# A linear-attention block with a gated MLP on one core: the rest of q formed beside k, the reciprocal denominator spread by DMA, the gate's tiles on 128 rows around the folds, and the last tile in column parts

## The chip, the cores and the metric

The kernel runs on one core of one Trainium2 chip. The time is the device time of that core in microseconds (us), as a median of several runs. The "span" that the profile gives is the profiled part of one run, and it is 1.7 to 2.2 us shorter than that run's time. A run of one kernel that is over 1.5% above the fastest of that kernel counts as slow and is left out of comparisons.

Names of engines in the profile: PE is the matrix engine, PEld its weight loads, DVE the vector engine, ACT the scalar engine, POOL the third elementwise engine, SP the engine whose queue issues most DMAs (SPq is that queue). SBUF is the memory that the kernel's tiles lie in, up to 128 partitions each, PSUM the banks that its matmuls write.

## The reference, cut to what matters

```
B, S, D, F, H = 1, 2048, 448, 1792, 16        # head size Dh = 28, bf16

xn = layernorm(x)

# A: linear attention
q, k, v = heads(xn @ wqkv)
phi     = lambda t: where(t > 0, t + 1, exp(t)) + 1e-6
kv      = einsum("bhsd,bhse->bhde", phi(k), v)
z       = einsum("bhsd->bhd", phi(k))
num     = einsum("bhqd,bhde->bhqe", phi(q), kv)
den     = einsum("bhqd,bhd->bhq", phi(q), z) + 1e-6
s       = (num / den) @ wo

# B: the gate
g   = silu(relu(xn @ w1 + b1) ** 2 @ w2 + b2)

out = x + s * g
```

`den` has one number per token and head. It divides the 28 features of that head, so 1/den has to be spread from 16 heads to 448 features before it can multiply phi(q).

## The kernel before

The program lists its operations in the order in which PE is to run them, and a small scheduler places those of the other engines. D = 448 is 3 x 128 + 64 rows, so a product over D takes seven steps of 64 rows. The kernel runs two products at once, one on the upper and one on the lower 64 rows (in the trace, at L852, the second of two such matmuls starts 0.003 us after the first, and 28 of them, 448 columns each, take 2.65 us). A `phase` is such a pair of products; `K4` and `K3` are the four and three steps of a half:

```
half = (slice(0, 64), slice(64, 128), slice(0, 128))
K4, K3 = (3, 0, 1, 2), (0, 1, 2)
...
def kk(si):                       # k of one tile of 128 tokens: 448 columns
    ...
        return e.matmul(
            ps(b)[:, 0:D], xT[half[h], c, si * P : (si + 1) * P], w_qkv[half[h], c, D : 2 * D], start=start,
            stop=stop,
        )
...
def q_rest(pair):                 # q's features 384..447, two groups of 512 tokens, a product of its own
    ...
        for i in (0, 1):
            g = 2 * pair + i
            last = e.matmul(
                ps(b)[half[i], 0:512], w_qkv[half[h], c, 384:448], xT[half[h], c, g * 512 : (g + 1) * 512],
                start=start, stop=stop,
            )
```

`den()` leaves the denominators of four groups of 512 tokens in a PSUM bank, group g at partitions 32g to 32g+15, one head per partition. ACT makes 1/den of it (`rden`, a log and an exponential). Then PE spreads it: `spread` multiplies `rden` with a matrix of zeros and ones, and DVE multiplies phi(q) with the result.

```
def spread(*what):
    ...
        for h, (g, r) in enumerate(what):
            w = ehd[half[h], g % 2, r * P : (r + 1) * P] if r < 3 else ehr[half[h], :, :]
            last = e.matmul(ps(bufs[h])[:, 0:512], w, rden[half[h], :], start=True, stop=True)
    ...
    add("pe", f, ["rden", "ehd", "ehr"], bufs, 0.22)
    for (g, r), b in zip(what, bufs):
        ...
        add("dve", lambda e, _, sl=sl, b=b: e.tensor_tensor(out=sl, in0=sl, in1=ps(b)[:, 0:512], op=ALU.mult), ...)
```

`fold_wv` and `fold_wo` fold the state kv with the weights, so that s becomes one product of phi(q)/den with `msb`: `ss` (called an S phase here). `gg` is the gate's second product, over F = 14 x 128 rows (called g). The order on PE, cut:

```
r0, r1 = q_rest(0), q_rest(1)
phase((r0, K4), (r1, K4))
phase((r1, K3), (r0, K3))
token_sum(0); z_heads(); token_sum(1); den(); token_sum(2); token_sum(3); fold_wv()
...
phase((h8, K4), (h11, K4))
spread(*todo.pop(0))
phase((h9, K4), (h12, K4))
...
phase((ga, A), (gb, A))
spread(*todo.pop(0))
phase((ga, B), (gb, B))
...
ss_columns(15, 0)
ss_columns(15, 1)
```

## Time and profile before

| What | Value |
|---|---|
| time, median of the first 3 runs | 147.88 us (147.73 to 148.08) |
| span of the profiled run | 146.1 us |
| PE busy | 141.3 us, 97% |
| PE waits in the whole run | 1.3 us, one, at the start |
| first hidden-layer matmul to last matmul | 9.65 to 142.5 us, without a gap |

The page of the kernel before: busy time by engine, the rows of PE and of its granted clock in 40 slices of the span (9 is 90% or more), and the chain of waits by engine.

```profile
PE 141.3 (97%) x1330; PEld 69.2 (47%) x1330; DVE 97.2 (67%) x224; ACT 79.8 (55%) x154; POOL 21.2 (14%) x39
...
PE   6999999999999999999999999999999999999990
...
PEclk9999999999999999999999999999999999999999
...
PE 93%; DVE 3%; DMA 2%; issue 0%; DVEq 0%
```

The waits of PE in the kernel before (engine and line, what it waited for; total us, times, longest):

```profile
PE pb L966 <- DVE junk L341: 1.3, 1, 1.3
```

Read together, these say that the matrix engine bounds the kernel. The chain that ended last is PE work for 93% of the span, PE has one short wait, and its clock is on record as full (1.00) from 5.6 to 145.5 us, past its last matmul, which ends at 142.8. By this profile, shortening DVE or ACT would gain nothing; taking matmuls away would.

The groups of instructions by form in the kernel before (line, engine, operation, shapes, count; busy us and mean ns of one; idle time before them):

```profile
L601 PE MATMUL pb<-w_qkv,xT 64*128 64x448 bf16 x100 | 14.6, 349 | 0.0
...
L839 DVE TENSOR_TENSOR pqT<-pqT,pb 128x512 bf16<-128x512 bf16 x12 | 7.7, 684 | 3.1 <-PE pb L830 3.1
...
L830 PE MATMUL pb<-rden,ehd 64*128 64x512 bf16 x12 | 2.3, 376 | 0.0
...
L638 PE MATMUL pb<-xT,w_qkv 64*64 64x512 bf16 x28 | 1.9, 383 | 0.1
```

L601 is k, L638 the separate product of q's rest, L830 the spreading of 1/den, and L839 the DVE product that uses it. The mean of one matmul (349 ns) is not its cost on PE, because matmuls overlap. From start to start in the trace, a 448-column matmul takes 0.189 us, one of 512 columns 0.216, and a change of tile shape to or from one with 64 or 32 rows or columns adds about 0.094 (a 448-column matmul before such a change takes 0.283).

The chain of waits of the kernel before, between 66 and 83 us (start, us, what):

```profile
66.06 1.02 PE pb L638 x16
...
67.12 0.84 PE pb L638 x12
67.97 3.13 PE pb L683 x16
...
78.55 1.63 PE pb L689 x16
...
82.20 0.22 PE pb L830 x2
```

The rest of q costs 1.02 + 0.84 us of the chain, and each pair of spreading matmuls 0.22.

### The profile page before, as it was taken

The numbers are of one execution on the slowest core, as the hardware profiler recorded it, in microseconds if no ns is written. First come the engines' busy times: TensorE is split into PE (matmuls) and PEld (weight loads), VectorE is DVE, ScalarE is ACT, GpSimd is POOL, SyncE is SP. The second block draws the span as 40 slices with busy tenths as digits, with TensorE's granted clock in tenths as the row PEclk, the third lists the DMA queues.
The fourth block names the chain that finished last, engine by engine and source line by source line (L and its number), as shares of the span: only waits on it lengthen the run. The fifth ranks groups of instructions, "written<-read, shape, count | busy, mean of one in ns | idle before, by whom it ended". The sixth has DMA issues, their size and how long they took to land.

```text
span 146.1 us, 3240 instructions
## 1 busy us (share of the span) xinstructions
PE 141.3 (97%) x1330; PEld 69.2 (47%) x1330; DVE 97.2 (67%) x224; ACT 79.8 (55%) x154; POOL 21.2 (14%) x39
## 2 busy tenths in 40 slices
PE   6999999999999999999999999999999999999990
PEld 2344446644444446443545535545555555555440
DVE  0979688888978995999995594973052341604583
ACT  3557799889887888889797191613030220301310
POOL 6000000000000000008900000000050505144140
PEclk9999999999999999999999999999999999999999
DMA  4997649995301100000000000000001011020122
GB/s 124 307 332 215 161 88 350 307 204 112 72 4 36 36 4 0 0 0 4 0 0 0 4 0 0 7 0 0 0 17 51 31 36 63 0 65 2 63 94 94
DMA packets 15513, 10.54 MB, mean 72 GB/s; under 512 B 7244, under 2 KB 15116, under 8 KB 15500
## 3 DMA queue, kind: packets, MB, share of 16 engines
q1 hardware_dynamic: 15040, 9.89, 26.5%
q10 hardware_dynamic: 460, 0.46, 0.9%
q8 instruction: 10, 0.16, 0.5%
q14 instruction: 3, 0.02, 0.1%
HBM read 6.94 MB, written 1.84 MB: 60 GB/s over the span
## 4 chain that ended last, share of the span: by engine, by line
PE 93%; DVE 3%; DMA 2%; issue 0%; DVEq 0%
PE pb L651 29%; PE pb L852 29%; PE pb L601 7%; PE pb L912 7%; PE pb L683 6%; PE pb L623 6%; DMA x_tok<-in_A_x_dram 2%; PE pb L638 1%; DVE st L447 1%; PE pb L689 1%; PE pb L830 1%; PE pb L775 1%; PE pb L741 1%; PE pb L803 1%; PE pb L930 1%; PE pb L490 1%
## 5 line engine op out<-in xcount | busy, mean ns | idle before, releaser
L651 PE MATMUL pb<-xT,w 64*128 64x512 bf16 x392 | 51.6, 376 | 0.1
L852 PE MATMUL pb<-w,r 64*128 64x448 bf16 x448 | 48.2, 349 | 0.0
L660 ACT ACTIVATE r<-pb,b1f 128x512 bf16<-128x512 f32 x56 | 35.0, 689 | 9.0 <-PE pb L651 8.9
L852 PEld LDWEIGHTS pb<-w,r 64*128 64x128 bf16 x448 | 22.8, 94 | 21.0 <-PE pb L852 0.6
L651 PEld LDWEIGHTS pb<-xT,w 64*128 64x128 bf16 x392 | 21.7, 94 | 21.7 <-ACT r L660 0.7
L870 ACT ACTIVATE gbuf<-gbuf 128x448 bf16<-128x448 bf16 x15 | 8.3, 577 | 35.7 <-DVE gbuf L860 35.7
L860 DVE TENSOR_TENSOR gbuf<-pb,b2b 128x448 bf16<-128x448 f32 x15 | 8.7, 621 | 25.4 <-PE pb L852 25.4
L899 POOL TENSOR_TENSOR obuf<-obuf,x_tok 128x448 bf16<-128x448 bf16 x12 | 12.1, 1029 | 57.4 <-DVE obuf L889 57.4
L601 PE MATMUL pb<-w_qkv,xT 64*128 64x448 bf16 (+1 forms) x106 | 16.0, 350 | 0.0
L623 PE MATMUL pb<-xT,w_qkv 64*128 64x512 bf16 x84 | 15.6, 376 | 0.0
L668 DVE TENSOR_TENSOR r<-r 128x512 bf16<-128x512 bf16 x37 | 13.7, 443 | 0.0
L912 PE MATMUL pb<-msb,pqT 64*128 64x448 bf16 x90 | 13.6, 349 | 0.0
L669 ACT ACTIVATE r<-r 128x512 bf16<-128x512 bf16 x19 | 11.3, 633 | 0.0
L447 DVE BATCH_NORM_STATS2 st<-x_tok 128x6 f32<-128x448 bf16 x16 | 9.4, 611 | 2.5 <-DMA x_tok<-in_A_x_dram 2.5
L889 DVE TENSOR_TENSOR obuf<-pb,gbuf 128x448 bf16<-128x448 f32 (+1 forms) x17 | 9.6, 593 | 2.2 <-PE pb L852 1.7
L579 ACT ACTIVATE pk<-pb 128x448 bf16<-128x448 f32 x16 | 8.1, 540 | 3.6 <-PE pb L601 2.9
L591 DVE SCALAR_TENSOR_TENSOR pk<-pb,pk 128x448 bf16<-128x448 f32 x16 | 9.8, 622 | 0.4
L378 POOL MEMSET ehd<- 128x896 bf16 x1 | 0.8, 844 | 62.9 <-DVE zb L613 62.9
L839 DVE TENSOR_TENSOR pqT<-pqT,pb 128x512 bf16<-128x512 bf16 x12 | 7.7, 684 | 3.1 <-PE pb L830 3.1
L683 PE MATMUL pb<-pk,xn 128*128 128x448 bf16 x48 | 9.6, 353 | 0.0
L601 PEld LDWEIGHTS pb<-w_qkv,xT 64*128 64x128 bf16 (+1 forms) x106 | 6.8, 94 | 5.1 <-DVE xT L500 0.4
L623 PEld LDWEIGHTS pb<-xT,w_qkv 64*128 64x128 bf16 x84 | 6.3, 94 | 4.3
(90 smaller groups left out, 117.5 us busy)
## 6 DMA issues: line engine op xcount, KB each, us to landing
out_dram<-obuf SPq DMA_DIRECT2D x15, 112.0 KB, 1.7
w<-in_B_w_dram SPq DMA_DIRECT2D x1, 1568.0 KB, 9.5
x_tok<-in_A_x_dram SPq DMA_DIRECT2D x3, 448.0 KB, 4.4
w_qkv<-in_A_wqkv_dram SPq DMA_DIRECT2D x3, 336.0 KB, 4.8
w<-in_B_w_dram SPq DMA_DIRECT2D x2, 384.0 KB, 4.6
w<-in_B_w_dram SPq DMA_DIRECT2D x1, 576.0 KB, 5.7
w_o<-in_A_wo_dram SPq DMA_DIRECT2D x1, 392.0 KB, 10.8
w_qkv<-in_A_wqkv_dram SPq DMA_DIRECT2D x6, 56.0 KB, 4.3
```

The costliest lines, as they stand in the source:

```text
L447: "dve", lambda e, _: e.bn_stats(st6[:, si, :], x_tok[:, si, :]), [("x", si)], [("st", si)], 0.553
L591: lambda e, _: e.scalar_tensor_tensor(out=slot, in0=ps(buf)[0:rows, 0:n], scalar=1.0 + 1e-6, in1=slot, op0=ALU.add, op1=ALU.max),
L601: return e.matmul(ps(b)[:, 0:D], xT[half[h], c, si * P : (si + 1) * P], w_qkv[half[h], c, D : 2 * D], start=start, stop=stop,)
L623: return e.matmul(ps(b)[:, 0:512], w_qkv[half[h], c, m * P : (m + 1) * P], xT[half[h], c, g * 512 : (g + 1) * 512], start=start, stop=stop,)
L651: return e.matmul(ps(b)[:, 0:512], w_1[half[h], c, fi * P : (fi + 1) * P], xT[half[h], c, g * 512 : (g + 1) * 512], start=start, stop=stop,)
L660: lambda e, _: e.activation(out=slot, in_=ps(b)[:, 0:512], func=AF.Relu, bias=b1f[:, fi : fi + 1]),
L668: return e.tensor_tensor(out=slot, in0=slot, in1=slot, op=ALU.mult)
L669: return e.activation(out=slot, in_=slot, func=AF.Square)
L683: last = e.matmul(ps(b)[:, 0:D], xn[:, si, c * P : (c + 1) * P], pk[:, si, :], start=(si == 0), stop=(si == NT - 1),)
L852: return e.matmul(ps(b)[:, 0:D], r2[half[h], fi, si * P : (si + 1) * P], w_2[half[h], fi, :], start=start, stop=stop)
L899: eng, lambda e, _: e.tensor_tensor(out=ob, in0=ob, in1=x_tok[:, si, :], op=ALU.add),
L912: return e.matmul(ps(b)[:, 0:D], q, msb[half[h], k, :], start=start, stop=stop)
```

## The change

The intent is to take work off PE. There are four parts.

1. **q rest beside k.** The k product of a token tile gets 64 more columns, q's features 384 to 447. They come out with tokens on partitions, so a DMA transposes them, two tiles at a time. The separate q-rest product goes.
2. **1/den spread by DMA.** Four DMAs write `rden` to DRAM. Each reads 16 partitions (the 16 heads of a group) and repeats each row 28 times. Six DMAs read the result back as 128 partitions of features. The spreading matmuls go.
3. **g on 128 rows around the folds.** Where the neighbours are products on 128 rows, the gate's tiles 0 to 3, 14 and 15 also run on 128 rows, which avoids changes of tile shape at 0.094 us each.
4. **The last tile in column parts**, 256 and 192 columns, to shorten the end.

The diff, cut to its core:

```
 def kk(si):
-    ps(b)[:, 0:D], xT[half[h], c, si * P : (si + 1) * P], w_qkv[half[h], c, D : 2 * D], start=start,
-    stop=stop,
+    ps(b)[:, 0:512], xT[half[h], c, si * P : (si + 1) * P], w_qkv[half[h], c, 384 : 2 * D],
+    start=start, stop=stop,
...
+def rest_transpose(pair):
+    add("sp", lambda e, _: e.dma_start_transpose(out=pqR[:, pair * P : (pair + 1) * P], in_=qk[:, pair, 0:P]), ...)
...
-def q_rest(pair):
...
-def spread(*what):
...
+def scale_q():
+    for g in range(NG):
+        rows = rden[32 * g : 32 * g + NH, :]                                     # 16 partitions
+        rows = bass.AP(tensor=rows.tensor, offset=rows.offset, ap=[rows.ap[0], [0, DH], rows.ap[1]])   # each row 28 times
+        dma("sp", spread[:, g * 512 : (g + 1) * 512].rearrange("(h j) t -> h j t", h=NH), rows, [("spread", g)], D * 1024, ["rden"])
+    for g in range(NG):
+        dma("sp", rb[:, :, g * 512 : (g + 1) * 512], spread[0:384, g * 512 : (g + 1) * 512]..., [("rb", g)], 384 * 1024, [("spread", g)])
+        if g:
+            continue
+        for i in (0, 1):
+            dma("sp", rbR[half[i], :]..., by_parity(spread[384:448, :], i), [("rbr", i)], 64 * 2048, [("spread", k) for k in range(NG)])
+    for g in range(NG):
+        ...   # DVE: pqT *= rb (3 x 512 columns at once), pqR *= rbR
...
-r0, r1 = q_rest(0), q_rest(1)
-phase((r0, K4), (r1, K4))
-phase((r1, K3), (r0, K3))
+full(gg(0))
+full(gg(1))
+z_heads(); token_sum(0); den(); open_gates(); scale_q()
+token_sum(3); token_sum(1); token_sum(2)
+full(gg(2))
+fold_wv()
+full(gg(3))
...
+for i, *pairs in ((4, 0), (6, 2), (8, 4, 6), (10, 8), (12, 10, 12)):
+    ga, gb = gg(i), gg(i + 1)
+    ...
+    phase((ga, C), (gb, C))
+    phase((x, K4), (y, K4))       # the first S phase
...
+full(gg(15, ca))
+full(ss(15, ca, eng="dve", end=False), KS, ["msz"])
+full(gg(15, cb, True), range(NF + 1))
+full(ss(15, cb, eng="dve", end=False), KS, ["msz"])
```

The two small reads of `spread[384:448]` need all four writes, because they take the last 64 features of every token group. Every S phase needs the scaled rest of q, so every S phase needs the last of the four writes.

## The prediction

> What bounds the kernel. TensorE. The table of busy time has PE at 141.3 of 146.1 us (97%), the chain of waits is 93% PE, and PE's waits add up to 1.3 us, all at the start. From the first hidden-layer matmul (9.65 us) to the last matmul (142.5 us) PE never stops, at full granted clock. So only removed PE work, a shorter tail or a new PE stall can move the time; DVE (67%) and ACT (55%) have room.
>
> PE work, from start-to-start times in the timeline: a 448-column matmul 0.189 us, 512 columns 0.216, 224 columns 0.096, 112 columns 0.052, alike on 128 rows and on a pair of 64-row halves; a change of tile shape adds 0.094. [...]
>
> Removed: the separate q-rest product, 1.9 us (blocks of 1.02 and 0.84); seven pairs of broadcast matmuls, 7 x 0.216 = 1.5; about 0.2 of the z product; ten of sixteen shape switches, 0.9 (partly in the items above); small waits around the folds and the last tiles, 0.3 to 0.4. Added: k tiles of 512 instead of 448 columns, 56 slots x 0.027 = 1.5, 0.17 of it in the head; two half slots for tiles 14 and 15 on zero-padded weights, 0.2. These spacings applied to every matmul of both programs give -2.7 us after the head; with head and waits, PE ends 2.6 to 3.0 us earlier. The tail (142.6 to 146.1) shrinks 0.1 to 0.2. Net about -3.1 us: 144.8 if nothing stalls.
>
> Not on the path: q scaling on DVE (14 x 0.684 us become four 3x512 products of about 0.9); longer k evictions; removed POOL constants.
>
> What may stall. 1/den now goes through DRAM and back: four writes of 448 rows of 1 KB, each read from 16 partitions, then four reads of 384 KB and two small ones that need all the writes. 1/den is there near 83 us, and the first S phase should start near 99.3. At 46 ns per 1 KB packet and engine (the trace's own reads) everything lands by 96, some 2 us to spare. [...] I hold the stall a little less likely than not.
>
> Prediction: 145.2 us, range 144.2 to 152.0; faster by over 2% 0.36, within 2% 0.37, slower by over 2% 0.27. The no-stall case lies on the 2% line.
>
> What would show each step: PE matmuls 1330 to 1215; q-rest and broadcast groups gone; no PE idle before the first S matmul (right), or a wait there on DVE's scaled q, itself on the DMA into rb (wrong); [...] DVE's min-add on k still near 270 ns; tail near 3.3 us.
>
> Wrong if: the DRAM round trip is late; DVE or ACT fall behind in the k phases so that PE waits for PSUM banks; the DMA transposes of q rest delay the next xT.

The sum without a stall came to 144.8 us. The case with a stall came to 151 to 153 us; all its terms were worked out from a transfer rate that no DMA of the trace of before showed. The stated 145.2 us lies between the two cases, near the first.

## The result, and the profile after

| | before | after |
|---|---|---|
| time, median | 147.98 us (147.73 to 148.15, 4 runs) | 155.84 us (154.85 to 157.19, 4 runs, the 157.19 slow) |
| ratio of fast runs | | 1.051 (95%: 1.048 to 1.055), slower |
| span of the profiled run | 146.1 us | 153.1 us |
| mean granted clock of PE | 0.998, full until 145.5 us | 0.965 |

Ratios in this document are the mean time of one kernel's fast runs over the mean of the other's fast runs of the same rounds, to within 0.0002, so they are not quite the ratio of the medians beside them. The outputs of every experiment were correct.

The page of the changed kernel, the same parts as before, with its line of DMA issues for the new writes at the end (KB each, median us from issue to landing):

```profile
PE 140.3 (92%) x1215; PEld 67.6 (44%) x1215; DVE 91.2 (60%) x218; ACT 78.9 (52%) x151; POOL 23.5 (15%) x37
...
PE   6999999999999999999999999900899999999992
...
PEclk9999999999999999999999999975589999999999
...
PE 80%; DMA 12%; SPq 4%; DVE 1%; ACT 1%; issue 0%; DVEq 0%
...
spread<-rden SPq DMA_DIRECT2D x4, 448.0 KB, 13.1
```

The matmuls went down from 1330 to 1215 as planned. But the row of PE now has two slices of nothing, the row of the clock reads 7, 5, 5, 8 from the first of these slices on, and the chain of waits holds 12% DMA and 4% of the issuing queue, where it had 2% and none.

The waits in the changed kernel, of DVE and of PE:

```profile
DVE pqT L850 <- DMA xT<-spread: 12.6, 2, 11.2
...
PE pb L955 <- DVE pqR L856: 8.4, 1, 8.4
...
PE pb L994 <- DVE junk L345: 1.3, 1, 1.3
```

Apart from the 1.3 us at the start, PE waits once, for 8.44 us, at the first S phase (L955), for DVE's scaled rest of q (`pqR`). DVE itself had waited for the DMA that reads `spread` back (into the space of `xT`). So the engine named in PE's wait is not the cause; the DMA behind it is. DVE's queue adds to it: its scaling of the first group waited 11.2 us for a read that landed at 104.83, and the copies of the folded weights, which the S phase needs too, stood behind it and ended at 107.41.

The chain of waits of the changed kernel across that stall (start, us, what):

```profile
82.19 0.64 ACT rden L819
...
84.30 3.89 SPq L393
...
88.23 15.52 DMA spread<-rden
...
103.76 0.57 SPq L393
...
104.37 3.10 DMA xT<-spread
...
107.50 0.30 DVE pqR L856
...
107.85 1.68 PE pb L955 x8
109.52 3.84 PE pb L889 x28
```

1/den is ready at 82.8 us. The fourth write is issued at 88.23 and lands 15.52 us later, at 103.75. The small reads are issued at 103.76 and 104.37; the second lands at 107.47. DVE scales in 0.30 us and PE starts at 107.85.

The instructions of the tile `rden` in the changed kernel (operation, count, shortest/median/longest ns, first and last start):

```profile
L393 SPq DMA_DIRECT2D spread<-rden x4: 659/2301/4611, 82.8 to 88.2; - x4
...
DMA to landing us min/median/max: 7.1/13.1/15.5
```

The four writes in the trace, one by one:

| write | issued (us) | landed (us) | after the one before (us) |
|---|---|---|---|
| group 0 | 82.84 | 89.94 | |
| group 1 | 83.55 | 94.62 | 4.68 |
| group 2 | 84.30 | 99.50 | 4.88 |
| group 3 | 88.23 | 103.75 | 4.25 |

The mean spacing is 4.60 us for 458,752 bytes, which is 100 GB/s.

The table of windows for the changed kernel: the stall and the first S and g phases after it. After the window and its length come busy time and count of PE, PEld, DVE, ACT and POOL, then the granted clock, the DMA share, and GB/s:

```profile
99.30:107.85 8.55, 0.11 (x3) 0.01 (x2) 2.85 (x5) 0.58 (x1) 0.00 (x0) 0.63 0.71 147
107.85:113.80 5.95, 5.95 (x44) 2.64 (x46) 4.15 (x9) 0.00 (x0) 0.00 (x0) 0.67 0.48 158
```

99.30 is where the first S phase could have started (the last matmul before the stall starts at 99.06, and the repaired kernel below starts S at 99.30 exactly). In the second window PE is busy all the time but at a granted clock of 0.67. In the trace the clock is at half from 101.58 to 111.82 us. This profiled run (154.85 us) is the fastest of the fast three; the other two, 0.9 and 1.1 us longer, left no trace.

### The profile page after: what moved, and what is told of

Its sections match the earlier page's. It is cut to its first block, busy times and chain, and to the rows that moved or that the text cites. A ratio compares the mean times of both kernels' runs of the same rounds, so it can differ in the third digit from the quotient of the medians.

```text
span 153.1 us, 3012 instructions
## 1 busy us (share of the span) xinstructions
PE 140.3 (92%) x1215; PEld 67.6 (44%) x1215; DVE 91.2 (60%) x218; ACT 78.9 (52%) x151; POOL 23.5 (15%) x37
## 4 chain that ended last, share of the span: by engine, by line
PE 80%; DMA 12%; SPq 4%; DVE 1%; ACT 1%; issue 0%; DVEq 0%
PE pb L640 28%; PE pb L889 23%; DMA spread<-rden 10%; PE pb L597 8%; PE pb L955 8%; PE pb L628 6%; SPq L393 4%; PE pb L994 3%; DMA xT<-spread 2%; PE pb L672 2%; PE pb L487 1%; ACT lnd L815 0%; PE pb L488 0%; PE pb L803 0%; ACT rden L819 0%
## 5 line engine op out<-in xcount | busy, mean ns | idle before, releaser
L889 PE MATMUL pb<-w,r 64*128 64x448 bf16 (+3 forms) x378 | 46.3, 351 | 0.0
L889 PEld LDWEIGHTS pb<-w,r 64*128 64x128 bf16 (+1 forms) x378 | 23.0, 97 | 21.3 <-issue 2.7
L900 DVE TENSOR_TENSOR gbuf<-pb,b2b 128x448 bf16<-128x448 f32 (+1 forms) x16 | 9.3, 608 | 31.4 <-PE pb L889 31.4
L934 POOL TENSOR_TENSOR xn<-xn,x_tok 128x448 bf16<-128x448 bf16 x15 | 15.1, 1033 | 59.2 <-DVE xn L925 59.2
L597 PE MATMUL pb<-w_qkv,xT 64*128 64x512 bf16 (+1 forms) x106 | 17.6, 376 | 0.0
L955 PE MATMUL pb<-msb,pqT 64*128 64x448 bf16 (+3 forms) x93 | 11.8, 358 | 0.0
L585 DVE SCALAR_TENSOR_TENSOR qk<-pb,qk 128x512 bf16<-128x512 f32 x16 | 10.6, 686 | 0.2
L575 ACT ACTIVATE qk<-pb 128x512 bf16<-128x512 f32 x16 | 9.0, 594 | 3.3 <-PE pb L597 2.7
L955 PE MATMUL pb<-msb,pqR 64*128 64x448 bf16 x14 | 2.7, 378 | 8.4 <-DVE pqR L856 8.4
L925 DVE TENSOR_TENSOR xn<-pb,gbuf 128x448 bf16<-128x448 f32 (+2 forms) x17 | 9.3, 589 | 1.9 <-ACT gbuf L865 1.5
L672 PE MATMUL pb<-qk,xn 128*128 128x448 bf16 x48 | 9.4, 353 | 0.0
```

Of the source, the lines that this page charges most:

```text
L585: lambda e, _: e.scalar_tensor_tensor(out=slot, in0=src(), scalar=1.0 + 1e-6, in1=slot, op0=ALU.add, op1=ALU.max),
L597: return e.matmul(ps(b)[:, 0:512], xT[half[h], c, si * P : (si + 1) * P], w_qkv[half[h], c, 384 : 2 * D], start=start, stop=stop,)
L672: last = e.matmul(ps(b)[:, 0:D], xn[:, si, c * P : (c + 1) * P], pk_of(si), start=(si == 0), stop=(si == NT - 1),)
L889: return e.matmul(ps(b)[:, 0:n], r2[half[h], fi, si * P : (si + 1) * P], w_2[half[h], fi, c], start=start, stop=stop)
L934: eng, lambda e, _: e.tensor_tensor(out=ob, in0=ob, in1=x_tok[:, si, c], op=ALU.add),
L955: return e.matmul(ps(b)[:, 0:n], q, m, start=start, stop=stop)
```

## The experiments

The leading theory was that a DMA whose source lies in 16 partitions is limited by the SBUF side, so that the writes come late, PE waits, and its clock drops. The expectations call it the port theory; that is a name only, as no run shows what in the SBUF side sets the rate. The rivals were that the repeated source rows, the 4 KB row pitch of the DRAM tensor, or the many 1 KB packets make the writes slow, and that the time was lost in other parts of the change (wider k, transposes, DVE). For the second part of the loss, a lowered clock stood against a plain wait.

### e_bench: the disputed transfer by itself

The kernel before, with nine extra DMAs one after the other on the SP queue while that queue is otherwise quiet. Their results go to scratch tensors. The sketch of the edit:

```
+bench: source rows of x_tok, 1 KB each -> DRAM
+  pitched    16 partitions, 28 times each, rows 4 KB apart in DRAM (as in the change)
+  tight      16 partitions, 28 times, rows packed
+  every8th   16 partitions that lie 8 apart, 28 times
+  thirtytwo  32 partitions, 14 times      sixtyfour 64 partitions, 7 times      all 128 partitions, 4 times
+  distinct   16 partitions, 14 different rows each (224 KB)
+  source     16 partitions, once (16 KB)
+  fromdram   those 16 rows in DRAM, 28 times
```

> The kernel before, with nine extra transfers on the sync queue while the DMA engines are idle, each waiting for the landing of the one before; all but two move 448 rows of 1 KB to DRAM. Rows come from: 16 partitions read 28 times to a destination of 4 KB row pitch (the change's own write); the same to packed rows; 16 partitions 8 apart; 32 partitions; 64 partitions; 128 partitions (512 rows); 16 partitions with 14 different rows each (224 rows); then 16 rows from DRAM read 28 times. Port theory [...]: about 4.5 us of transfer plus 2 us fixed for the first two (6 to 7 us to landing), about half the transfer for 16 partitions 8 apart, 32 and 64 (4 to 5 us), about 1.5 us plus 2 for 128 partitions (3.5 us), the distinct rows as slow per byte as the repeated ones (4 to 4.5 us for half the bytes). Row pitch theory: the packed destination lands in 4 us or less, partitions make no difference. Repeat theory: the distinct rows are fast (3 us), the 28 reads from DRAM are slow.

The time was 148.65 us (one run). The page's DMA issues in e_bench (KB each, us from issue to landing):

```profile
b_all<-x_tok SPq DMA_DIRECT2D x1, 512.0 KB, 3.2
b_pitched<-x_tok SPq DMA_DIRECT2D x1, 448.0 KB, 6.7
b_tight<-x_tok SPq DMA_DIRECT2D x1, 448.0 KB, 6.5
b_every8th<-x_tok SPq DMA_DIRECT2D x1, 448.0 KB, 4.0
b_thirtytwo<-x_tok SPq DMA_DIRECT2D x1, 448.0 KB, 4.1
b_sixtyfour<-x_tok SPq DMA_DIRECT2D x1, 448.0 KB, 4.1
b_fromdram<-b_source SPq DMA_DIRECT2D x1, 448.0 KB, 3.5
...
b_distinct<-x_tok SPq DMA_DIRECT2D x1, 224.0 KB, 4.1
...
b_source<-x_tok SPq DMA_DIRECT2D x1, 16.0 KB, 2.3
```

All of these have 1 KB packets. The pitch in DRAM makes 0.2 us (6.7 against 6.5). The repeats are not the cause either: 224 KB of different rows from 16 partitions take 4.1 us, as long as 448 KB of repeated rows from 32 partitions. What matters is which partitions are read: 16 neighbours 6.5 us, 16 partitions 8 apart 4.0, 32 neighbours 4.1, 64 neighbours still 4.1. The single packets, in the packed trace's DMA records, say the same: the median 1 KB packet took 140 ns from 16 neighbours (139 with different rows), 72 from 16 partitions 8 apart, 72 from 32 and from 64, and 46 from 128 partitions and from DRAM. Each transfer ran once.

Counted from the start of the first packet to the end of the last, the transfers ran at 93 GB/s from 16 neighbours, 185 from 16 that lie 8 apart, 181 from 32 and 181 from 64. At 93 GB/s the packets take about 4.9 of the 6.5 to 6.7 us; the other 1.6 to 1.8 us stand where the expectation had "2 us fixed". Why 16 partitions that lie 8 apart are as fast as 32 neighbours, and 64 no faster, is not shown.

### e_ports32: twice as many source partitions

The changed kernel, with each head's 1/den in two neighbouring partitions. `zmask` already widened each denominator column to 32 columns of which 16 were used; the new pattern fills all 32, so the matmuls and ACT instructions stay the same. Each write then reads 32 partitions, 14 times each.

```
-band("zmask", zmask[:, 0:4, :], [[P, 4], [-DH, 32]], 0)
+twice = lambda v: v.rearrange("p c (h r) -> p c h r", r=2)
+band("zmask", twice(zmask[:, 0:4, :]), [[P, 4], [-DH, 16], [0, 2]], 0)
...
-rows = rden[32 * g : 32 * g + NH, :]          ... ap=[rows.ap[0], [0, DH], rows.ap[1]]
+rows = rden[32 * g : 32 * g + 2 * NH, :]      ... ap=[rows.ap[0], [0, DH // 2], rows.ap[1]]
```

> The changed kernel with each head's 1/den held in two neighbouring partitions, so that each of the four writes reads 32 partitions, 14 times each; same bytes, same destination, same order, no instruction added. Port theory: each write takes about 2.4 us instead of the measured 4.7, the fourth lands near 95 us instead of 103.7, no wait before the first S matmul, clock stays full, about 145 us (144.5 to 146). Rival (destination pitch, number of rows, DRAM side): landing near 103 us and about 155.5 us as before the edit.

It took 144.37 us (144.28 to 144.9), just under the 144.5 to 146 expected, ratio to before 0.976 (0.973 to 0.979): faster. Tile `rden` of e_ports32, as shown above for the changed kernel:

```profile
L394 SPq DMA_DIRECT2D spread<-rden x4: 625/1270/2212, 82.9 to 86.2; - x4
...
DMA to landing us min/median/max: 4.3/6.9/8.3
```

The waits of PE in e_ports32:

```profile
PE pb L995 <- DVE junk L345: 1.3, 1, 1.3
PE pb L488 <- DVE xn L467: 0.2, 1, 0.2
```

Its table of windows over the same work, the first S and g phases:

```profile
99.30:103.30 4.00, 4.00 (x46) 2.07 (x44) 3.35 (x7) 0.00 (x0) 0.00 (x0) 1.00 0.57 193
```

The writes land at 87.19, 89.64, 92.09 and 94.52, 2.45 us apart (188 GB/s), and the small reads at 97.38 and 98.26. DVE has scaled the rest of q by 98.6, and S starts at 99.30 without a wait. The same S and g phases take 4.00 us instead of 5.95.

This closes the account of the two profiled runs. Their spans differ by 153.1 - 142.6 = 10.5 us; the stall is 8.55 us from 99.30 to 107.85, and the slow phases after it cost 5.95 - 4.00 = 1.95 us more. The sum is 10.5, so nothing else separates these two kernels. Both hold the other parts of the change; whether one of those loses time is asked by e_pe_spread, e_qrest_apart and e_tail_whole.

### e_ports128: one write from all partitions

The same doubling of partitions, and a single write of all 1792 KB from 128 partitions instead of four; the small reads become four pieces, because the layout in DRAM changes.

```
-spread = nc.dram_tensor("spread", [D, S], bf, kind="Internal").ap()
+spread = nc.dram_tensor("spread", [NG * D, 512], bf, kind="Internal").ap()
...
-for g in range(NG): ... four writes of 448 KB
+dma("sp", spread.rearrange("(q j) t -> q j t", q=P), rows_of_all_128, ..., NG * D * 1024, ["rden"])
```

> As e_ports32, with the rows of all four token groups put one after the other in DRAM, so that one transfer reads all 128 partitions, 14 times each. Port theory: 1.8 MB land within about 7.5 us of the issue (near 90.5 us), the first read back near 92.5; no wait of PE, about 144.9 us (144.5 to 145.5), no better than e_ports32 if that one has no wait either. Rival (total of bytes written): near 103 us as before, about 155 us.

It took 144.72 us (144.5 to 145.18), ratio 0.978 (0.975 to 0.982). The write is issued at 82.80 and lands at 90.22, 7.42 us for four times the bytes. The first large read lands at 93.41 and the small ones by 95.06. PE does not wait. So the time gained at the writes, more than 4 us over e_ports32, is worth nothing: both are early enough.

### e_keepwarm: the same stall, with PE kept busy

The changed kernel, with 40 matmuls on unused data added, one to claim a PSUM bank and 39 before the first S phase. They fill the stall and feed no result. If the whole loss were the wait, nothing would change; if the clock has a part in it, that part comes back.

```
+hold = Buf("W")
+add("pe", junk_mm(1), ["junk"], [hold], 0.216)
...
     phase((ga, C), (gb, C))
+    if i == 4:
+        add("pe", junk_mm(39), ["junk", hold], [hold], 39 * 0.216)
     x, y = us[0]
```

> The changed kernel with 39 junk matmuls of 512 columns (8.4 us) ahead of the first S matmul, where PE waits 8.4 us; the result is unchanged. If the halved clock after the wait costs what the trace suggests (S and g phases after it 5.5 us instead of 3.4, so 2.1 to 2.4 us), it gives 153.2 us (152.7 to 153.8) with the wait itself unchanged; if the clock costs nothing, 155.5 us.

It took 153.15 us (153.08 to 153.37), ratio to before 1.035 (1.032 to 1.038). The writes land as late as before (89.72 to 103.57). The table of windows for e_keepwarm, the stretch of the stall and the 4.00 us behind it:

```profile
99.30:107.85 8.55, 8.55 (x43) 3.74 (x39) 2.81 (x5) 0.58 (x1) 0.00 (x0) 1.00 0.74 155
107.85:111.85 4.00, 4.00 (x44) 2.00 (x44) 2.92 (x8) 0.00 (x0) 0.00 (x0) 1.00 0.67 219
```

The second window begins with the end of the added matmuls: the first S phase starts at 108.03, 0.18 us later than in the changed kernel. From there its S and g phases take 3.98 us at full clock, where the changed kernel took 5.92 at a mean of 0.67. The lowered clock is therefore a cost of its own: 1.94 us in this stretch of the profiled runs (their spans differ by 1.8, as S started later), and about 2.6 us between the medians of fast runs (155.70, the middle one of 154.85, 155.70 and 155.99, against 153.15). In the changed kernel half clock is recorded from 2.3 us after PE stopped at 99.3 until 4.0 us after it restarted; in e_fill_wait below, from 3.4 us after the stop until 3.5 us after the restart. Why these times differ is not shown.

### e_ports32_again: the repaired kernel in the next rounds

No edit; it is there so that the next three experiments have the repaired kernel beside them on the same chip.

> The kernel of e_ports32 once more, as the base of the three others of this call: 144.4 us, ratio 0.976 to the kernel before.

It took 144.39 us (144.14 to 145.67), ratio 0.977 (0.974 to 0.981). The result repeats, though the interval now crosses 0.98.

### e_pe_spread: the repaired kernel with the spreading back on PE

The 0/1 matrix and the spreading matmuls of the kernel before, put into the order of the changed kernel; everything else of the change stays.

```
-scale_q()
+spread_pe(r, (0, 2))   # pairs after token_sum(1) and after gg(2)
+spread_pe(r, (1, 3))   # pairs in the first two 64-row g phases
```

> The changed kernel with 1/den spread by broadcast matmuls on PE again (eight pairs, from a 0/1 matrix) and everything else of the change kept. No transfer to wait for. From the spacings of the trace of before, applied to its list of matmuls: 2.3 us more PE work than e_ports32 (eight pairs 1.7, six or so tile shape switches more). Theory (the transfers cost only the wait, and without it save the PE work they replace): 146.6 us (146.2 to 147.2). Rival (something else of the change is slow too): over 148 us.

It took 146.86 us (146.78 to 147.05), ratio to before 0.993 (0.992 to 0.995). That is 2.5 us above e_ports32_again; the expectation was 2.3. Against this placement of the pairs, with the changes of tile shape that it brings, the DMA spread is worth 2.5 us where it lands in time, which makes it the largest part of the gain. The other parts, without the DMA, bring 147.87 - 146.86 = 1.0 us.

### e_qrest_apart: the repaired kernel with the rest of q as its own product

k is back at 448 columns, the q-rest product is back on PE (writing the new layout), and the transposes go.

```
-    ps(b)[:, 0:512], xT[...], w_qkv[half[h], c, 384 : 2 * D],
+    ps(b)[:, 0:D], xT[...], w_qkv[half[h], c, D : 2 * D],
...
-    rest_transpose(2 * g)
-    rest_transpose(2 * g + 1)
 late_constants(["zb"])
+r0, r1 = q_rest(0), q_rest(1)
+phase((r0, K4), (r1, K4))
+phase((r1, K3), (r0, K3))
```

> e_ports32 with the q rest as a product of its own again, written straight in the new layout of pqR (k tiles 448 columns wide, no DMA transposes). From the spacings: q rest 1.9 us, k tiles 1.5 us less, so 0.4 us slower than e_ports32 (0.2 to 0.8): 144.8 us. If the wider k tiles, their longer evictions or the eight transposes cost something that the sum leaves out, it is faster than e_ports32.

It took 145.26 us (145.03 to 145.4), ratio 0.982 (0.980 to 0.984), 0.87 us above e_ports32_again, a little over the 0.2 to 0.8 expected. The part is a small gain: 1.9 us of product removed, against wider k tiles. The trace shows nothing against the transposes; in the changed kernel they land in 2.4 us in the median, and PE does not wait for them.

### e_tail_whole: the repaired kernel with the last tile in one piece

```
-full(gg(15, ca))
-full(ss(15, ca, eng="dve", end=False), KS, ["msz"])
-full(gg(15, cb, True), range(NF + 1))
-full(ss(15, cb, eng="dve", end=False), KS, ["msz"])
-store(15, [ca, cb], "act")
+full(gg(15, call, True), range(NF + 1))
+full(ss(15, call, eng="dve", end=False), KS, ["msz"])
+store(15, [call], "act")
```

> e_ports32 with the last tile in one piece of 448 columns, bias still by matmul. From the durations of the trace: finish on 448 instead of 192 columns 0.62 instead of about 0.37 us, residual 0.38 instead of 0.26, the silu in front of it 0.58 instead of 0.35 (partly under the last S matmuls), so 0.3 to 0.6 us slower than e_ports32: 144.8 us. If the tail is hidden or set by the store alone: the same time as e_ports32.

It took 144.92 us (144.45 to 145.39), ratio 0.980 (0.977 to 0.982). The interval overlaps that of e_ports32_again (0.974 to 0.981). The profiled spans are 142.7 and 142.8 us, and the last store is issued 0.1 us later than in the profile of e_ports32. This is inconclusive: the column parts may be worth anything from nothing to half a microsecond.

### e_from_dram: the 16 rows read from DRAM instead of SBUF

The changed kernel with its 16 rows and 28 repeats per write. Only the source moves: `rden` is first stored once (128 KB), and the four writes read that copy.

```
+once = nc.dram_tensor("once", [P, 512], bf, kind="Internal").ap()
...
+dma("sp", once[:, :], rden[:, :], ["once"], P * 1024, ["rden"])
 for g in range(NG):
-    rows = rden[32 * g : 32 * g + NH, :]
+    rows = once[32 * g : 32 * g + NH, :]
```

> The changed kernel, but the 1/den rows are first stored once (128 rows, 128 KB, all partitions), and the four writes of 448 rows then read them from DRAM instead of from 16 partitions: same destination, pitch, row size, count and order, one transfer more in front. Port theory: the store 2.3 us, the four writes about 1.5 us each after it, the fourth lands near 94 us, no wait before the first S matmul, 144.5 to 145.2 us. Rival (the writing side of the four transfers is what is slow): the fourth lands at 106 us or later and the time is 157 us or more.

It took 144.26 us (144.12 to 144.34), just under the 144.5 to 145.2 expected, ratio 0.975 (0.973 to 0.976): faster. The instructions of the tile `once` in e_from_dram:

```profile
L394 SPq DMA_DIRECT2D spread<-once x4: 614/622/623, 84.9 to 86.9; - x4
L394 SPq DMA_DIRECT2D once<-rden x1: 353/353/353, 82.9 to 82.9; - x1
...
DMA to landing us min/median/max: 2.0/6.6/7.1
```

The store lands after 2.04 us, and all four writes have landed by 94.06, 9.1 us after the first was issued, although a whole DMA was added in front of them. The number of rows, the repeats, the 1 KB packets, the pitch and the destination are those of the changed kernel. So the delay belongs to reading from these 16 partitions of SBUF, not to the shape of the transfer. The issues are short again too: 0.62 us each, where the changed kernel's third and fourth took 3.89 and 4.61.

### e_fill_wait: other work in the stall

The changed kernel, with a g phase moved ahead of the first S phase. If the start of S is set by a landing, moved work fits into the wait for nothing.

```
+    if i == 4:
+        phase((gb, C), (ga, C))
     phase((x, K4), (y, K4))
-    phase((gb, C), (ga, C))
+    if i > 4:
+        phase((gb, C), (ga, C))
```

> The changed kernel with one g phase of 28 matmuls (2.65 us) moved from behind the first S phase to in front of it, so that PE works in the first part of the wait; the transfers are as in the change. The start of the first S matmul stays near 107.9 us, set by the landings; the wait falls from 8.4 to about 5.8 us, and 2.65 us of work (4.0 at the halved clock it ran at) leave the stretch behind it: 152.0 us (151.5 to 153.2). If the wait moved with the work (PE or DVE order was its cause, not the transfers), 155.5 us.

It took 153.72 us (153.2 to 155.16), ratio to before 1.041 (1.035 to 1.046), 1.7 us above the 152.0 expected. The waits of PE in e_fill_wait:

```profile
PE pb L955 <- DVE pqR L856: 6.6, 1, 6.6
```

The wait shrank by 1.8 us rather than by the whole phase that was moved in, because S started at 108.94 and not at 107.85. The landings were later as well (fourth write 104.19 rather than 103.75, second small read 108.57 rather than 107.47). The clock was at half from 105.59 to 112.41, so the S phases paid for it again. The part that the theory needs held: the start of S follows the landing of the small read by 0.4 us in both kernels. The size missed, because both the landing and the lowered clock were taken too kindly. Why the transfers landed later in this run was not tested.

## Why the prediction was wrong

The prediction said 145.2 us with a range of 144.2 to 152.0. The result was 155.84. Point by point:

- **PE bounds the kernel; less PE work shortens it: right.** Its sum without a stall was 144.8. The repaired kernel takes 144.4, with the first S phase at 99.30 as predicted. The 0.4 us between are in the profile: the last matmul ends 3.2 us earlier (142.8 to 139.6) rather than 2.6 to 3.0, and the end behind it is 0.3 us shorter rather than 0.1 to 0.2.
- **"At 46 ns per 1 KB packet and engine (the trace's own reads) everything lands by 96": this step failed.** Those packets were reads from DRAM into 128 partitions, and the trace of before had no DMA out of 16 partitions. The number was read from the profile, yet it was a number for another transfer: in the changed kernel the median 1 KB packet of these writes took about 150 ns. They ran at 100 GB/s. The last write landed at 103.75 and the last small read, which PE needs, at 107.47, not by 96. The stall, held "a little less likely than not", was what happened.
- **The case with a stall was the right mechanism, put too small.** It came to 151 to 153 us, and the result was 155.84. In the changed kernel the first write landed after 7.1 us and the others 4.25 to 4.88 us apart, so the last came at 103.75. The small reads landed at 106.67 and 107.47, and the wait was 8.4 us.
- **The lowered PE clock was a term of that case without a size.** It measured 1.95 us in the profiled runs and about 2.6 in the medians.
- **The stalled case of 151 to 153 and the upper end of 152.0 did not fit together.** With nearly even chances for the stall, the range cut through its own second case. Two outcomes 7 us apart call for a range that holds both, or a firm choice.
- **The other dangers did not come.** PE had no wait on PSUM banks. The transposes did not delay it. DVE's four products with 1/den took 0.95 us each, where about 0.9 was said, and its minimum-and-add on k stayed near its 0.27 us. In the groups of the changed kernel it reads

```profile
L578 DVE TENSOR_SCALAR qk<-qk 128x512 bf16<-128x512 bf16 x16 | 4.6, 290 | 5.2 <-ACT qk L575 5.2
```

  and in those of the kernel before

```profile
L584 DVE TENSOR_SCALAR pk<-pk 128x448 bf16<-128x448 bf16 x16 | 4.3, 272 | 5.6 <-ACT pk L579 5.6
```

  so 14% more columns took 7% more time.
- **A measurable sign it named caught the failure.** It said that a wait before the first S matmul, on DVE's scaled q and through it on the DMA, would mean that it was wrong. That wait was there, 8.44 us at L955. The landing of the first write took 7.1 us in the changed kernel and 4.3 in the repaired one.

What stays open: whether the three repaired kernels (32 partitions 144.4, 128 partitions 144.7, source in DRAM 144.3) differ at all, as PE waits in none of them beyond the start; what the column parts of the last tile are worth; what g on 128 rows brings by itself, which no run isolated.

The version to keep is e_ports32, or e_from_dram, which is as fast: 144.3 to 144.4 us, 2.3% to 2.5% below the kernel before.

## What to carry to other kernels

In these runs the time of a DMA followed where its source lay and not its bytes alone: 448 KB took 6.5 us from 16 neighbouring partitions, 4.0 from 16 that lie 8 apart and 3.5 from DRAM. So before a DMA replaces matmuls, look at which partitions it reads and compare it with a measured transfer of the same kind, not with the reads that the trace happens to hold. If few partitions hold the data, put copies in idle rows of an instruction that runs anyway, or store it once and read it from DRAM; either turned 5% slower into 2.4% faster here. And when a bounding matrix engine may have to wait for microseconds, add what a lowered clock after the wait may cost (here 4.0 us at half clock after a wait of 8.4 us cost 1.95 us), and let the range hold that case whole.
